# Issuing the exchanges of q's half-row maxima and sums on GpSimd's queue, with another order for the second plan

## The chip, the cores and the metric

The kernel runs on one core of a Trainium2 chip. The metric is the device time in microseconds (us) of one execution. A core has five engines that run side by side, each in its own program order, and wait for one another through semaphores: TensorE (PE, matrix products; its weight loads are shown apart as PEld), VectorE (DVE), ScalarE (ACT), GpSimd (POOL) and SyncE (SP), which here only starts transfers. A transfer can be started by SP, ACT or POOL; "issue" below is the time that the starting engine spends on it, "landing" is the time from the issue to the arrival of its data.

## The reference

```python
def _attn_ref(q, k, v):                       # each 8 x 8 x 576 x 64 (batch, head, sequence, head_dim)
    q_s = np.exp(q - np.max(q, axis=-1, keepdims=True))
    q_s = q_s / (np.sum(q_s, axis=-1, keepdims=True) + 1e-09)
    k_s = np.exp(k - np.max(k, axis=2, keepdims=True))
    k_s = k_s / (np.sum(k_s, axis=2, keepdims=True) + 1e-09)
    kv = np.einsum('bhsd,bhse->bhde', k_s, v)
    return np.einsum('bhsd,bhde->bhse', q_s, kv)

def _moe_ref(x, w_in, w_out):                 # x 4608 x 512, w_in 512 x 2048, w_out 2048 x 512
    h = np.maximum(x @ w_in, 0.0)
    return h * h @ w_out
```

The attention's output, with the heads side by side, is the x of the second function.

## The kernel before, in words

**Work and stages.** The 4,608 rows are nine tiles of 512 tokens. Tile 0 is the first plan's (to about 130 us). Tile 1 (about 130 to 219 us) is a plain feed-forward tile: for each of 16 blocks of the hidden width a product `h` (four slices of x with a block of w_in), on ScalarE and VectorE relu, square and a split in a high part `gh` and a low part `gl`, and then four accumulating products `acc` with w_out. From 219 to about 650 us five steps run two tiles' worth of rows with sums of blocks of w_in and x, so that fewer products are needed; the sums of w_in (`w_sums`) are read from device memory through two buffers, `ring_0` and `ring_1`, with SP's queue. For one pair of hidden blocks the ring loads are a first one of 768 KB into one ring buffer, two of 256 KB, and one of 512 KB. PE multiplies the ring blocks with x sums (`w0` ... `w5`) into two banks, `h_2_0_0` and `h_2_0_1`; ScalarE copies the bank to `u0`, `u1`, `u2`, and only then may PE write the next product into it. The last stage (650 to 805.5 us) is a joint one.

`ring_0` has the memory that `x0` of tile 1 had, so its first load waits for PE's last product that reads `x0_1`: the first six of `h_1_15`. `ring_1` has that of `x1_1`.

**The attention beside it.** While PE multiplies for one tile, the other engines make the attention's output for the next, one pair of heads `p` at a time (four pairs in a batch element `b`). For b of 2 and more q is loaded in blocks of 32 columns: four loads of 72 KB put the two halves of each 64-wide row on different partitions. So each partition has the maximum and the sum of half a row:

- `blocks_exp` takes the half row's maximum (into `bst[:, 0]`), subtracts it and takes the exponential on ScalarE;
- `blocks_swap` sums the half row on VectorE (into `bst[:, 1]`) and starts four transfers of 32 partitions by 36 numbers (4.5 KB), which bring each partition its partner's maximum and sum (into `bst[:, 2:4]`);
- `blocks_norm`, the merge, has VectorE wait for them, then two small VectorE operations, a small exponential on ScalarE, four small VectorE operations and the scaling of q.

There are 24 such exchanges (6 batch elements by 4 pairs), so 96 transfers, all in the second plan.

**The order of work.** The program does not run in the order in which its functions are called. Every operation is recorded as a node (`Engine.tell`, which is why nearly every row of the profile says L101), and `Planner.order` writes the nodes out again: at each step it takes the engine that could start soonest, and on it the node with the largest `tail`, an urgency. `shift` is called once for each number of a list and adds a random amount to the tails of up to 40 nodes in a row; the list thus selects one order out of many:

```python
r = random.Random(seed)
at, size, by = r.randrange(len(self.nodes)), r.randint(1, 40), r.gauss(0.0, 5.0)
for n in self.nodes[at:at + size]:
    n.tail += by
```

`SEEDS` is the list for the first plan, `LATER` that for the second, which has everything from tile 1 to the joint stage.

Of the kernel before, what the change touches and what calls it, by code (L numbers as in the profile page):

```python
# [381 lines left out]
def attention_ffn(  # L382
# [64 lines left out]
    )  # L447
    EASE = 0.0
    EARLY = 2
# [36 lines left out]
    V, S, G = Engine(plan, nc.vector, 0.14, 0.00108, port=2), Engine(plan, nc.scalar, 0.18, 0.00087), Engine(plan, nc.gpsimd, 0.1, 0.0021, 0.23, 1)  # L486
    T, Y = Engine(plan, nc.tensor, 0.013, 1 / 2400, port=None), Engine(plan, nc.sync, 0.1, 0.0)
# [260 lines left out]
    def blocks_swap(b, p):  # L748

        st = made["bst", b, p]  # L750
        V.tensor_reduce(out=st[:, 1, :].only("sum"), in_=made["q", b, p], op=ALU.add, axis=AX.X, n=SQ)
        for j in range(2):
            for a in range(2):
                at, of = j * D + a * Q, j * D + (1 - a) * Q
                Y.dma_start(
                    out=st[at:at + Q, 2:4, :].only(at),
                    in_=st[of:of + Q, 0:2, :].only("max", "sum"), kb=1,
                )
        made["swap", b, p] = True
# [697 lines left out]
    def prepare(b, p, begin=True):  # L1457

        k_max(b, p)
        if b >= TB:  # L1460
            k_reduce(b, p)
            if begin:
                blocks_exp(b, p)
                if p:
                    blocks_swap(b, p)
            k_shift(b, p, made.pop(("kmx", b, p)), V)
            return
        q_max(b, p, G)
        if p == 0:
            tail_exp(b)  # L1470

    def step(b, s):

        p, i = divmod(s, NP)
        if b >= TB:
            if i == 0:
                if ("bst", b, p) not in made:
                    blocks_exp(b, p)
                if ("swap", b, p) not in made:
                    blocks_swap(b, p)  # L1480
            elif i == 1:
                blocks_norm(b, p)
        elif i == 0:
            k_turn_max(b, p)
            q_exp(b, p)
            q_norm(b, p, G)
            if p == 0:
                tail_norm(b)
# [852 lines left out]
```

## Time and profile before

| | before |
|---|---|
| time, median of 3 runs (lowest to highest) | 806.51 us (806.22 to 807.58) |
| the profiled execution | 807.3 us |
| its span, first to last instruction | 805.5 us |
| mean granted TensorE clock | 0.997 |
| instructions | 14938 |

The span is what the profile sees; 1.8 us of the execution lie around it. PE is busy nearly throughout and its clock stays at the upper level, so the reading looks for the few places at which PE stands still, and for what it waits there.

### The profile page before, as it was taken

Reading aid. Unit: us, or ns where it says so; the run is one execution under the profiler, and the core shown is the slowest. Engines: PE = TensorE matmul, PEld = TensorE weight load, DVE = VectorE, ACT = ScalarE, POOL = GpSimd, SP = SyncE. Lnnn points to the kernel's source line nnn. Section 1 sums busy time; section 2 is a strip of 40 time slices with the busy share of each in tenths; the row PEclk is TensorE's granted clock in tenths of the full one; section 3 lists DMA queues with packets and bytes.
Section 4 is the critical chain, followed back from the end, with each engine's and each line's share of the span. In section 5 each row is a group of like instructions: output and inputs, shape, how many; then the busy total and the mean of one; then the engine's idle time right before and its main releaser. Section 6 shows DMA issues by size and latency. Waiting matters only on the chain.

```text
span 805.5 us, 14938 instructions
## 1 busy us (share of the span) xinstructions
PE 786.8 (98%) x5189; PEld 690.0 (86%) x5189; DVE 598.7 (74%) x1252; ACT 497.6 (62%) x967; POOL 138.7 (17%) x165
## 2 busy tenths in 40 slices
PE   7989999999989999999999999999999999999997
PEld 6668788888888989989898989898989888888887
DVE  6878896778767878777887776778786663346995
ACT  5887864545655667575657666666665665566442
POOL 4888893000000000000000000000000000000005
PEclk9999999999999999999999999999999999999999
DMA  9994115955598989898889888889899469999565
GB/s 270 382 319 158 41 40 166 297 172 154 136 284 248 276 253 292 243 271 242 266 256 265 265 218 267 239 277 261 264 269 271 130 211 353 374 330 381 168 183 101
DMA packets 210890, 193.19 MB, mean 240 GB/s; under 512 B 127424, under 2 KB 172992, under 8 KB 210816
## 3 DMA queue, kind: packets, MB, share of 16 engines
q1 hardware_dynamic: 205824, 189.96, 77.3%
q10 hardware_dynamic: 4352, 1.51, 0.8%
q0 software_dynamic: 640, 0.79, 0.5%
q8 instruction: 41, 0.67, 0.3%
q14 instruction: 33, 0.27, 0.1%
HBM read 150.34 MB, written 41.29 MB: 238 GB/s over the span
## 4 chain that ended last, share of the span: by engine, by line
PE 85%; DMA 6%; SPq 3%; DVE 2%; ACT 1%; issue 1%; POOL 1%; ACTq 0%; POOLq 0%; DVEq 0%
PE acc L101 34%; PE h L101 31%; PE h L1354 9%; PE out L2087 6%; PE kv L101 4%; SPq L101 3%; DMA q<-in_q_dram 1%; DMA raw<-in_moe_w_out_dram 1%; DMA raw<-in_moe_w_in_dram 1%; DMA ring<-w_sums 1%; DMA k<-in_k_dram 1%; ACT w L101 1%; DVE w L101 1%; PE x L101 1%; POOL out_dram L101 1%
## 5 line engine op out<-in xcount | busy, mean ns | idle before, releaser
L101 PE MATMUL acc<-w,gh 128*128 128x512 f32 x888 | 266.9, 382 | 3.6 <-ACT o L101 1.8
L101 PEld LDWEIGHTS acc<-w,gh 128*128 128x128 f32 x888 | 154.2, 190 | 23.9 <-issue 4.8
L101 PE MATMUL acc<-w,gl 128*128 128x512 f32 x444 | 168.3, 379 | 0.0
L101 PEld LDWEIGHTS h<-w,ring 128*128 128x128 f32 x1200 | 152.6, 191 | 12.3 <-issue 2.4
L101 PE MATMUL h<-w,ring 128*128 128x256 f32 x1200 | 155.1, 276 | 1.2 <-DVE c L101 0.8
L101 DVE TENSOR_TENSOR c<-h,u 128x256 f32<-128x256 f32 (+1 forms) x144 | 66.9, 467 | 86.6 <-ACT u L101 48.6
L101 ACT ACTIVATE c<-c 128x256 f32<-128x256 f32 (+1 forms) x198 | 116.2, 587 | 22.3 <-DVE c L101 19.1
L101 ACT COPY u<-h 128x256 f32<-128x256 f32 (+1 forms) x144 | 58.6, 407 | 93.7 <-PE h L101 77.7
L101 POOL PARTITION_ALL_REDUCE kmx<-km x24 | 20.2, 840 | 456.3 <-DVE km L101 392.9
L101 PEld LDWEIGHTS acc<-w,gl 128*128 128x128 f32 x444 | 83.9, 189 | 12.0 <-DVE gl L101 0.2
L101 PE MATMUL h<-x,w 128*128 128x512 f32 x384 | 90.6, 383 | 1.1 <-DVE x L101 0.6
L101 PEld LDWEIGHTS h<-x,w 128*128 128x128 f32 x384 | 71.3, 189 | 13.9 <-issue 1.7
L2087 PE MATMUL out<-w,w 128*128 128x512 f32 (+1 forms) x370 | 72.7, 352 | 0.2 <-DVE o L101 0.2
L2087 PEld LDWEIGHTS out<-w,w 128*128 128x128 f32 x370 | 62.7, 190 | 7.8 <-DVE o L101 0.4
L101 DVE TENSOR_TENSOR gl<-c,gh 128x512 fp32r<-128x512 f32 x80 | 55.1, 690 | 13.8 <-ACT gh L101 12.8
L101 PEld LDWEIGHTS h<-w,w 128*128 128x128 f32 x480 | 59.8, 191 | 3.4 <-issue 0.8
L101 PE MATMUL h<-w,w 128*128 128x256 f32 x480 | 61.2, 276 | 0.0
L101 ACT CAST gh<-c 128x512 fp32r<-128x512 f32 x80 | 49.4, 619 | 2.2
L1354 PE MATMUL h<-w,ring 128*128 128x512 f32 x204 | 46.4, 380 | 0.8 <-ACT u L101 0.8
L101 DVE TENSOR_REDUCE bst<-q 128x18 f32<-128x576 f32 x48 | 35.9, 748 | 13.0 <-DMA q<-in_q_dram 9.1
L1354 PEld LDWEIGHTS h<-w,ring 128*128 128x128 f32 x204 | 38.5, 189 | 6.6 <-ACT u L101 1.2
L101 POOL TENSOR_TENSOR w<-w,w 128x512 fp32r<-128x512 f32 x32 | 41.1, 1295 | 5.9 <-ACT w L101 5.8
(183 smaller groups left out, 1087.1 us busy)
## 6 DMA issues: line engine op xcount, KB each, us to landing
ring<-w_sums SPq DMA_DIRECT2D x48, 768.0 KB, 5.9
w<-w_sums SPq DMA_DIRECT2D x48, 512.0 KB, 5.1
ring<-w_sums SPq DMA_DIRECT2D x90, 256.0 KB, 4.6
k<-in_k_dram SPq DMA_DIRECT2D x32, 256.0 KB, 4.6
raw<-in_moe_w_in_dram SPq DMA_DIRECT2D x16, 512.0 KB, 8.6
raw<-in_moe_w_out_dram SPq DMA_DIRECT2D x16, 512.0 KB, 9.6
w<-wo_sums SPq DMA_DIRECT2D x32, 256.0 KB, 3.9
g_b<-c SPq DMA_DIRECT2D x30, 256.0 KB, 5.5
```

The lines of the kernel that those rows point to most:

```text
L101: getattr(self.eng, op)(*map(real, args), **{k: real(a) for k, a in kwargs.items()})
L1354: nc.tensor.matmul(out=out.real(), lhsT=a[:, k * P:(k + 1) * P].real(), rhs=in_turn(m[k]).real(), start=(begin and k == 0 and i == 0), sto ...
L2087: nc.tensor.matmul(out=banks[name][m][:, at].real(), lhsT=a[:, m * P:(m + 1) * P].real(), rhs=(rhs if half is None else rhs[:, half]).real ...
```

## The change

The four transfers of an exchange are started by GpSimd (`G`) in place of SyncE (`Y`), and `LATER` has 27 more numbers:

```diff
@@ LATER
-        1730000948, 1730000978,
+        1730000948, 1730000978, 2220000000, 2220000002, 2220000005, 2220000010, 2220000017, 2220000021,
...
+        2220000287, 2220000317, 2220000402, 2220000438, 2220000516,
@@ blocks_swap
                 at, of = j * D + a * Q, j * D + (1 - a) * Q
-                Y.dma_start(
+                G.dma_start(
                     out=st[at:at + Q, 2:4, :].only(at),
                     in_=st[of:of + Q, 0:2, :].only("max", "sum"), kb=1,
```

Both edits change the order that the planner writes out, on all engines. Three places of it follow. A name ends in the tile or batch element, the pair or block, and a running number that may differ between the two orders.

PE at the end of tile 1, around the last product that reads `x0_1`; before, four rows of `kv` products of attention pairs (2,2) and (2,3) stand between the two halves of `h_1_15`:

```order
L101 MATMUL h_1_15_2465<-x0_1_1603,w14_1474 128x512 x6
L101 MATMUL kv_2_2_2331<-qT_2_2_2248,kv_2_2_2397 64x512
L101 MATMUL kv_2_3_2342<-qT_2_3_2471,kv_2_3_2400 64x512
L101 MATMUL kv_2_2_2331<-qT_2_2_2248,kv_2_2_2397 64x512
L101 MATMUL kv_2_3_2342<-qT_2_3_2471,kv_2_3_2400 64x512
L101 MATMUL h_1_15_2465<-x1_1_1619,w14_1474 128x512 x6
```

The same place after the change:

```order
L101 MATMUL kv_2_2_2335<-qT_2_2_2227,kv_2_2_2410 64x512
L101 MATMUL kv_2_3_2346<-qT_2_3_2435,kv_2_3_2433 64x512
L101 MATMUL kv_2_2_2335<-qT_2_2_2227,kv_2_2_2410 64x512
L101 MATMUL kv_2_3_2346<-qT_2_3_2435,kv_2_3_2433 64x512
...
L101 MATMUL h_1_15_2481<-x0_1_1603,w14_1474 128x512 x6
L101 MATMUL h_1_15_2481<-x1_1_1619,w14_1474 128x512 x6
```

The `kv` rows have moved ahead of the accumulating products of block 12, so that nothing stands between the halves of `h_1_15`.

SP's queue from the first ring load on; `w_sums_0` to `w_sums_2` are the sums of w_in, 128x1536 is the load of 768 KB and 128x512 one of 256 KB. Before:

```order
L101 DMA ring_0_2479<-w_sums_0_1607 128x1536
L101 DMA q_3_0_2488<-in_q_dram 32x18x32 x4
L101 DMA ring_0_2479<-w_sums_0_1607 128x512
L101 DMA ring_1_2527<-w_sums_0_1607 128x512
L101 DMA k_3_1_2531<-in_k_dram 128x2x256
L101 DMA w_sums_4_1822<-sums_i4_1_2416 128x2x256
L101 DMA ring_1_2527<-w_sums_1_1614 128x1536
L101 DMA v_3_1_2566<-in_v_dram 128x4x64 x2
L101 DMA ring_0_2479<-w_sums_2_1757 128x1536
L101 DMA ring_0_2479<-w_sums_1_1614 128x512
L101 DMA bst_3_0_2554<-bst_3_0_2554 32x36 x4
L101 DMA out_0_dram<-o_1_0_2617 128x512
```

And after:

```order
L101 DMA q_3_0_2448<-in_q_dram 32x18x32 x4
L101 DMA k_3_1_2485<-in_k_dram 128x2x256
L101 DMA ring_0_2498<-w_sums_0_1607 128x1536
L101 DMA ring_0_2498<-w_sums_0_1607 128x512
L101 DMA ring_1_2515<-w_sums_0_1607 128x512
L101 DMA ring_1_2515<-w_sums_1_1614 128x1536
...
L101 DMA ring_1_2515<-w_sums_1_1614 128x512
L101 DMA out_0_dram<-o_1_0_2630 128x512
L101 DMA q_3_1_2658<-in_q_dram 32x18x32 x2
L101 DMA out_0_dram<-o_1_2_2665 128x512
L101 DMA q_3_1_2658<-in_q_dram 32x18x32 x2
```

The loads of `q_3_0` have moved ahead of the first ring load, the exchange of pair (3,0) is gone from this queue, and two of the four loads of `q_3_1` stand behind the store of `o_1_2`. On GpSimd's queue the 24 exchanges alternate with the reductions of k's maxima (`kmx`), the only other work that it has in this part of the program.

ScalarE where pair (3,0) is merged (`ACTIVATE bst` is the merge's exponential; `o_1_0` and `o_1_2` are copies that empty the accumulators of tile 1, `acc_1_1` and `acc_1_3` here). Before:

```order
L101 COPY u2_2_0_2611<-h_2_0_0_2534 128x256
...
L101 COPY u0_2_1_2671<-h_2_0_0_2534 128x256
L101 ACTIVATE c0_2_0_2574<-c0_2_0_2574 128x512
L101 ACTIVATE bst_3_0_2554<-bst_3_0_2554 128x2x18
L101 COPY o_1_0_2617<-acc_1_1_1729 128x512
L101 CAST gh_2_0_2691<-c0_2_0_2574 128x512
L101 COPY o_1_2_2653<-acc_1_3_1745 128x512
```

And after:

```order
L101 COPY u1_2_0_2586<-h_2_0_0_2541 128x256
L101 ACTIVATE bst_3_0_2508<-bst_3_0_2508 128x2x18
L101 COPY u2_2_0_2623<-h_2_0_0_2541 128x256
...
L101 COPY u0_2_1_2684<-h_2_0_0_2541 128x256
L101 ACTIVATE c0_2_0_2584<-c0_2_0_2584 128x512
L101 CAST gh_2_0_2694<-c0_2_0_2584 128x512
L101 COPY o_1_0_2630<-acc_1_1_1736 128x512
L101 COPY o_1_2_2665<-acc_1_3_1751 128x512
```

The merge's exponential has moved from behind the first pair's square to a place ahead of the copy `u2_2_0`, and the cast `gh_2_0` to a place ahead of the copy of `acc_1_1`.

## Rows read from the trace of the kernel before

**Rows 1.** The page's busy times of the engines, with share of span and instruction counts.

```profile
PE 786.8 (98%) x5189; PEld 690.0 (86%) x5189; DVE 598.7 (74%) x1252; ACT 497.6 (62%) x967; POOL 138.7 (17%) x165
```

**Rows 2.** PE's waits, 118 to 660 us: us in total, times, longest.

```profile
PE acc L101 <- ACT o L101: 1.8, 1, 1.8
PE h L101 <- DVE c L101: 0.8, 1, 0.8
PE h L1354 <- ACT u L101: 0.8, 1, 0.8
PE h L101 <- DVE gl L101: 0.3, 1, 0.3
```

**Rows 3.** Tile bst, the exchanges' transfers: issue ns min/median/max; landing of all.

```profile
L101 SPq DMA_DIRECT2D bst<-bst x96: 507/588/1364, 138.5 to 624.2; - x96
...
DMA to landing us min/median/max: 1.7/4.0/7.2
```

**Rows 4.** SP's timeline, 213 to 241 us: start us, us, what was issued.

```profile
214.16 0.34 SPq L101 DMA_DIRECT2D ring<-w_sums  x1
214.59 3.78 SPq L101 DMA_DIRECT2D q<-in_q_dram  x4
218.41 1.14 SPq L101 DMA_DIRECT2D ring<-w_sums  x2
...
224.69 3.98 SPq L101 DMA_DIRECT2D bst<-bst  x4
```

**Rows 5.** Issues at 214.2, 218.5 and 224.7 us: KB each, median us to landing.

```profile
ring<-w_sums SPq DMA_DIRECT2D x1, 768.0 KB, 5.0
...
ring<-w_sums SPq DMA_DIRECT2D x1, 256.0 KB, 4.7
...
bst<-bst SPq DMA_DIRECT2D x4, 4.5 KB, 6.5
```

**Rows 6.** PE's timeline, 211 to 235 us: start, us, what [idle before, releaser].

```profile
218.85 0.38 PE L101 MATMUL acc<-w,gl 128*128 128x512 f32 x1
219.32 1.58 PE L101 MATMUL h<-w,ring 128*128 128x256 f32 x12
...
223.21 0.91 PE L101 MATMUL h<-w,ring 128*128 128x256 f32 x6 [0.34 <-DVE gl L101]
...
233.79 0.70 PE L101 MATMUL acc<-w,gh 128*128 128x512 f32 x2 [1.80 <-ACT o L101]
```

**Rows 7.** Chain of waits, 196 to 262 us: start us, us, what it was in.

```profile
210.24 2.59 PE acc L101 x12
...
214.13 1.02 PE kv L101 x8
...
254.64 1.34 PE h L101 x12
```

**Rows 8.** VectorE's timeline, 222 to 234 us: the sum of pair (3,0), the merge's start.

```profile
223.03 0.75 DVE L101 TENSOR_REDUCE bst<-q 128x18 f32<-128x576 f32 x1
...
232.59 0.41 DVE L101 TENSOR_TENSOR bst<-bst 128x18 f32<-128x18 f32 x2 [1.71 <-DMA bst<-bst]
```

**Rows 9.** ScalarE's timeline, 230 to 235 us.

```profile
230.98 0.64 ACT L101 ACTIVATE c<-c 128x512 f32<-128x512 f32 x1
...
233.18 0.57 ACT L101 COPY o<-acc 128x512 f32<-128x512 f32 x1
233.64 0.62 ACT L101 CAST gh<-c 128x512 fp32r<-128x512 f32 x1
```

**Rows 10.** POOL: output stores' issue ns; its reductions, 120 to 640 us; one of them; VectorE beside that.

```profile
L101 POOL DMA_DIRECT2D out_dram<-o x16: 584/584/907, 783.3 to 801.9; - x16
...
L101 POOL PARTITION_ALL_REDUCE kmx<-km x24 | 20.2, 840 | 456.3 <-DVE km L101 392.9 <-DVE v L101 26.6 <-DVE qtail L101 21.0
...
154.90 1.67 POOL L101 PARTITION_ALL_REDUCE kmx<-km  x1 [15.64 <-DVE km L101]
...
154.72 1.28 DVE L101 TENSOR_TENSOR full_i<-w 128x512 f32<-128x512 f32 x2
```

2 rows, old and new, of the table LATER are left out of this document.

## The prediction

> **What bounds the kernel now.** Read the busy times first [rows 1]: PE works 98% of the span, GpSimd 17%. Only PE's idle time, or work that PE has to do more, can move the end. So the second view is the list of PE's waits over the part of the program that the second plan orders and in which the exchanges lie, 118 to 660 us [rows 2]. The reader is to see how little it is: four waits, 1.8 + 0.8 + 0.8 + 0.3 = 3.7 us in 542. No order can win more than this there, 0.5% of the time; and every other exchange, however late, costs PE nothing now. I call a difference of up to 0.2% (1.6 us), about what a measurement of this kernel can tell from no change, "the same".
>
> The third step is to trace each wait to what caused it. The 1.8 us one is the exchange itself. SP issues the four transfers of pair (3,0) at 224.69, taking 3.98 us, behind several ring loads [rows 4]; they land 6.5 us after issue (a median over the four) where the median of all 96 is 4.0 [rows 3, 5]. VectorE, idle 1.71 us for them, starts the merge at 232.59 [rows 8], ScalarE's small exponential stands ahead of the copy that empties `acc_1_1` (233.18, [rows 9]), and PE, ready at 231.99, starts at 233.79 [rows 6]. The 0.3 us one, at 223.21 [rows 6], is labelled with a VectorE operation, but the product also needs the 256 KB ring load, issued at 218.41 behind four loads of q that hold SP for 3.78 us [rows 4], which lands 4.7 us later [rows 5]: 223.1. I take the load as its cause. The 0.8 us ones are the maximum of q_3_1, waiting for its loads ahead of an operation on `c`, at 246 us, and casts ahead of a copy to `u` at 654 us.
>
> **The change part by part.**
>
> *The issue itself.* SP is relieved of 96 issues of 0.588 us [rows 3]. GpSimd's nearest row is its own output stores: 0.584 us each, at most 0.907 [rows 10]. So an exchange takes GpSimd 4 x 0.584 = 2.3 us against SP's 2.4: equal. What is queued behind it on GpSimd is the next pair's reduction of k's maxima; GpSimd idles 456 us ahead of those 24 reductions [rows 10], so 24 x 2.3 = 56 us fit eight times over, and the k side is not what VectorE and PE wait for in [rows 2]. Cost 0; if the cover were gone, 2.3 us an exchange.
>
> *First ring load.* Before, x0's last product ends at 214.13 [rows 7], the load is issued at 214.16 [rows 4] and lands 5.0 us later [rows 5], 219.16. PE fills the time with the kv rows (1.02, [rows 7]), the second half of `h_1_15` and twelve acc products (2.59), is ready at 218.85 + 0.22 = 219.07 and starts at 219.32 [rows 6]: late by 0.25. Afterwards the kv rows stand ahead of x0's last product, so 1.02 us of cover is gone: six products of 0.215 (half of the 2.59 for twelve, 1.29) and the 2.59 are 3.9 us against 5.2 from release to start. Late by 1.3, so **+1.0**. Bounds: the q loads now stand ahead of the ring load, not behind it; landing of 4.0 (the median of exchanges) to 6.5 (the longest in these rows) gives 0 to +2.5.
>
> *Second ring load.* It now follows the first directly, without 3.78 us of q issues in between: due in time, **-0.3**. Bounds -0.3 to 0.
>
> *Exchange (3,0).* The loads of q_3_0 stand earlier, and the sum of the half rows is done by about 219.9 (ScalarE's exponential of q now stands ahead of the high part of `h_1_15`, which PE's ring products must follow closely; an estimate from the order and those times). GpSimd issues to 222.2, landing 2.0 to 4.0 later (between the shortest and the median of [rows 3]) gives 224.2 to 226.2. The merge's exponential stands ahead of the copy `u2_2_0`, and PE needs that copy's bank after the first pair's 30 h products (0.112 each, 1.34 for twelve) and 18 acc products (0.216 each): 7.25 us behind a start at 220.3, 227.5 [rows 7]. Take off two small VectorE operations (0.41, [rows 8]), the small exponential, the copy and the handing over, by estimate 1.1 in all: the merge may start as late as 226.4. It makes it, barely at 4.0: **-1.8**. Bounds: with landing 6.5, 228.7, it is 2.3 late: +0.5; so -1.8 to +0.5.
>
> *Copy of acc_1_1.* The cast `gh_2_0` now stands ahead of it. From the square's end (230.98 + 0.64 = 231.62, [rows 9]) the cast takes about 0.5 (its row says 0.62, of which some overlaps with its neighbours) and the copy 0.57: 232.7, against PE ready at 231.99. PE still waits, **+0.7** of the 1.8 removed. Bounds 0 to +1.8 (another operation ahead as now).
>
> *q_3_1 at 246 us.* Half its loads stand behind a store, and its exponential comes earlier on ScalarE. I cannot place its need better than at the 0.8 that it costs today: **0**, bounds -0.8 to +1.0 (a wait as long as the longest of [rows 2]).
>
> *The wait at 654 us, and the rest.* ScalarE's order before 654 us keeps the same casts: **0**. Between 250 and 650 us PE has no wait now, so a new order can only add: **0** taken, up to +3.6 (two waits as long as the longest of [rows 2]), since a few ring loads now stand behind others.
>
> *Sum:* +1.0 - 0.3 - 1.8 + 0.7 + 0 = -0.4. The profiled execution, 807.3 us, would be 806.9; it is 0.8 above the median of the runs shown (806.51), so the median would be 806.1.
>
> The landing is the weak spot of the exchange's term. Before, the exchange stood in one queue with SP's ring loads of 768 KB; afterwards it has a queue without them. The Trainium skill, page "DMA: Bandwidth & Descriptors", section "Queues, rings and completion order", says that each DMA engine takes turns between the queue rows it has work for, a packet at a time, so that small transfers on their own queue need not stand behind large ones; by it landing would be nearer 2 than 6.5, and the sum would stay at -0.4 with the merge 2 us ahead of its deadline. No run so far shows the exchanges on another queue.
>
> **The rivals.**
>
> *B: the transition clears.* One mechanism: the first ring load finds its queue empty and lands in 4.0, and the copy of acc_1_1 is in time because the pair's square runs earlier without the merge in the way. Terms: 0 - 0.3 - 1.8 + 0 = -2.1, with q_3_1 also earlier -0.8: -2.9, so 803.6 (804.4 without q_3_1). For it: three of the four waits of [rows 2] lie between 219 and 246 us. Against: the 5.0 landing had nothing ahead of it of its own tile.
>
> *C: the new order makes loads late elsewhere.* The same terms, but the first ring load lands in 6.0, between the 5.0 and 6.5 of [rows 5] (+1.0), and two later pairs wait for a ring load behind another (0.8 each, as [rows 2] has them): -0.4 + 1.0 + 1.6 = +2.2, so 808.7, slower. It decides once these added waits pass 2.0 us in all, the 0.4 gained and the 1.6 of the bound. For it: PE has no slack at all between waits. Against: SP has 96 issues fewer, so loads behind it go sooner.
>
> *D: GpSimd's issue is stretched beside VectorE.* One reduction on GpSimd took 1.67 us where the mean is 0.84 [rows 10], while VectorE ran operations with two inputs from SBUF (154.72, [rows 10]). Twice 0.584 is 1.17 an issue, 4.7 an exchange, and with landing 4.0 it is 8.7 us from sum to merge. Before, (3,0) had 8.8 (223.78 to 232.59) and cost 1.8, so 7.0 is free: it decides at 0.75 us an issue. At 8.7 each exchange is up to 1.7 late; if half of 24 cost that, +20; if three do, +5: 811 to 826. Against: 16 stores on GpSimd beside VectorE's last stage have a median of 0.584 and a maximum of 0.907. The Trainium skill, the same page, section "SWDGE vs HWDGE vs iDMA", has a rule against the change: GpSimd writes its descriptors itself, into memory that VectorE can lock it out of, while the hardware queues are spared that. By that rule the price is D's, 811 or more; the trace's stores do not show it.
>
> That the change does nothing is not a case: the order of all engines differs.
>
> **How the numbers follow.** The forecast (A, the same: 806.1, own range 804.9 to 807.6) 42%; B 30%; C 20%; D 8%. The likeliest is A. Faster by over 0.2% (under 804.9) holds B and a tail of A: 0.32. Slower (over 808.1) holds C, D less what C leaves inside the same: 0.26. The rest, 0.42, is the same. The range leaves out D and the outer tails of B and C: 803.3 to 809.0.
>
> **What would show each step.** In the profile after: GpSimd's issues of `bst` at 0.58 us, and landing of 2 to 4 us (steps one and three; 1.2 us or 6.5 us would make D or the failed term right). The first ring product waiting 1.3 us for the ring (+1.0 right) or none (B). At the copy of acc_1_1 a wait of 0.7 or none. At the second ring load no wait. PE's idle between 250 and 650 us, zero now, tells A from C at once. The prediction is wrong if PE's sum of idle in 118 to 660 us is under 2.1 or above 5.3 us, or if PE's work itself grows, which the order gives no reason for.

## The result, and the profile after

The changed kernel takes 812.55 us (median of 5 runs, 810.88 to 814.81) against 806.22 (5 runs, 803.34 to 807.58): a ratio of 1.0092, 95% interval 1.0071 to 1.0113. It is slower by 6.3 us, outside the range of the forecast. The profiled execution takes 814.0 us with a span of 812.2.

PE is not where the time went. The page's busy times after, which answer to [rows 1]:

```profile
PE 787.7 (97%) x5189; PEld 690.5 (85%) x5189; DVE 599.7 (74%) x1252; ACT 498.0 (61%) x967; POOL 186.6 (23%) x261
```

PE's waits from 118 to 660 us after, which answer to [rows 2]:

```profile
PE acc L101 <- ACT o L101: 1.0, 2, 0.8
PE h L101 <- DMA ring<-w_sums: 0.8, 1, 0.8
PE acc L101 <- DVE gl L101: 0.4, 1, 0.4
PE h L101 <- ACT kt L101: 0.4, 1, 0.4
PE h L1357 <- ACT u L101: 0.3, 1, 0.3
PE h L101 <- DVE c L101: 0.2, 1, 0.2
```

They add up to some 3.1 us, from 3.7. So the next view is PE's timeline at the very end; its last row before, and then after:

```profile
795.50 5.62 PE L2087 MATMUL out<-w,w 128*128 128x256 f32 x48 [0.22 <-DVE o L101]
```

```profile
794.90 5.62 PE L2090 MATMUL out<-w,w 128*128 128x256 f32 x48 [0.20 <-DVE o L101]
```

PE's last product ends at 801.12 before and at 800.52 after, 0.6 us earlier. In this execution PE was ahead by more than that before the changed part began (a row of 36 `h` products of tile 1 starts at 134.23 us against 135.63), so its later part is no faster. The span ends at 805.5 and at 812.2. Thus from PE's last product to the end it is 4.4 us before and 11.7 after: all of the loss, and a little more, lies where no product is left. What runs there belongs to the line that ends the program. Its instructions on GpSimd and SyncE (durations in ns, min/median/max; first and last start in us), before:

```profile
L2336 POOLq DRAIN  x3: 40/102/2824, 801.9 to 805.2; - x3
L2336 SPq DRAIN  x3: 7/7/7, 804.4 to 805.0; - x3
```

And after:

```profile
L2339 POOLq DRAIN  x3: 40/102/10148, 801.3 to 812.0; - x3
L2339 SPq DRAIN  x3: 7/7/7, 803.8 to 811.7; - x3
```

Each engine ends with a drain instruction, and all wait for one another behind it: SyncE's last drain starts at 805.0 before and at 811.7 after, 0.3 us behind the end of GpSimd's first. GpSimd's takes 2.82 us before and 10.15 after, 7.3 us more, while SyncE is through with its first at 803.8. The last store does not explain it. GpSimd's timeline has its issue beside the drain's start, at 801.31 after, and the trace has its data landed at 803.25, 8.2 us before the drain ends (at 811.44):

```profile
801.31 0.58 POOL L101 DMA_DIRECT2D out_dram<-o  x1 [2.10 <-DVE o L101]
```

The exchanges themselves, tile bst after (answers to [rows 3]):

```profile
L101 POOL DMA_DIRECT2D bst<-bst x96: 496/497/767, 137.1 to 624.9; - x96
...
DMA to landing us min/median/max: 1.5/4.4/6.7
```

An issue takes 0.497 us, less than SyncE's 0.588, and at most 0.767. Landing is 4.4 us in the median against 4.0.

Three rows of PE's timeline after show the moved places at the end of tile 1; they answer to [rows 6]:

```profile
218.67 1.57 PE L101 MATMUL h<-w,ring 128*128 128x256 f32 x12 [0.80 <-DMA ring<-w_sums]
...
222.76 0.94 PE L101 MATMUL h<-w,ring 128*128 128x256 f32 x6 [0.22 <-DVE c L101]
...
232.40 0.70 PE L101 MATMUL acc<-w,gh 128*128 128x512 f32 x2 [0.82 <-ACT o L101]
```

And VectorE's start of the merge of pair (3,0), which waits for nothing now (answers to [rows 8]):

```profile
223.92 0.41 DVE L101 TENSOR_TENSOR bst<-bst 128x18 f32<-128x18 f32 x2
```

### The profile page after: what moved, and what is told of

The parts are those of the page before. It is cut to its first block, busy times and chain, and to the rows that moved or that the text cites. A ratio compares the mean times of both kernels' runs of the same rounds, so it can differ in the third digit from the quotient of the medians.

```text
span 812.2 us, 14978 instructions
## 1 busy us (share of the span) xinstructions
PE 787.7 (97%) x5189; PEld 690.5 (85%) x5189; DVE 599.7 (74%) x1252; ACT 498.0 (61%) x967; POOL 186.6 (23%) x261
## 3 DMA queue, kind: packets, MB, share of 16 engines
q0 software_dynamic: 3712, 1.24, 0.8%
## 4 chain that ended last, share of the span: by engine, by line
PE 87%; DMA 4%; ACT 3%; SPq 1%; DVE 1%; issue 1%; POOL 1%; POOLq 0%; DVEq 0%; ACTq 0%
PE acc L101 34%; PE h L101 31%; PE h L1357 9%; PE out L2090 7%; PE kv L101 4%; DMA raw<-in_moe_w_out_dram 2%; DMA k<-in_k_dram 2%; SPq L101 1%; ACT c L101 1%; PE x L101 1%; ACT w L101 1%; ACT gh L101 1%; POOL out_dram L101 1%; DVE w L101 0%; ACT raw L101 0%
## 5 line engine op out<-in xcount | busy, mean ns | idle before, releaser
L101 POOL DMA_DIRECT2D bst<-bst x96 | 48.0, 506 | 266.1 <-DVE bst L101 229.7
L101 PEld LDWEIGHTS acc<-w,gl 128*128 128x128 f32 x444 | 83.9, 189 | 12.8 <-DVE gl L101 1.0
```

The source lines that it names most:

```text
L101: getattr(self.eng, op)(*map(real, args), **{k: real(a) for k, a in kwargs.items()})
```

## The experiments

**Theory one** after the first reading: GpSimd's drain retires every transfer that GpSimd issued, at a price for each, 7.3 us for 96 more; until the end of the program nobody pays it. "Retire" is only a name here for what the drain does about a transfer: no trace shows what that is, only how long it takes. **Rivals**: the new order delays the last stores; a fixed price once GpSimd issues transfers in mid-program; a price by packets or bytes. Four kernels test the first two, and three more the last.

*The new numbers without the move* (after):

```diff
-                G.dma_start(
+                Y.dma_start(
```

> The exchanges go back to SyncE's queue, the 27 new numbers stay. Theory one (the last instruction of GpSimd, a drain, must retire every transfer that GpSimd issued, so that its length grows with their number: 7.3 us for 96 more, 0.076 each): with 20 transfers on GpSimd the drain is 2.8 us as before, and the end lies 4.4 us behind PE's last product; time by PE's own waits, 804 to 807. Rival (the order that the new numbers give delays the last stores or their landing): the drain stays near 10 us and the time near 812.

Measured: 815.61 us, 1.0138 (1.0119 to 1.0157) of before. The drain:

```profile
L2339 POOLq DRAIN  x3: 40/93/2811, 811.5 to 814.8; - x3
```

It is 2.81 us, and the end follows PE's last product by 4.3 us: theory one holds and the rival of the late stores falls. The time was missed by 9 us, and PE shows why: from the first ring product to the first product of the joint output it takes 515.4 us (219.26 to 734.62), against 505.7 before (219.32 to 725.01) and 505.8 after (218.67 to 724.43). The 27 numbers, applied to nodes on other engines, give a third order and no part of the changed one.

*The move without the new numbers* (before):

```diff
-                Y.dma_start(
+                G.dma_start(
```

> The exchanges go on GpSimd's queue, the 27 new numbers are left out. Theory one: drain 10.1 us, some 7 us more than before, whatever PE's order gives; time 811 to 816. Rival (the new order): drain 2.8 us, time within 2 us of before.

Measured: 818.8 us, 1.018 (1.0155 to 1.0204).

```profile
L2336 POOLq DRAIN  x3: 40/102/10148, 805.7 to 816.3; - x3
```

The drain is that of after to the nanosecond, under another order. Here PE takes 510.6 us between the same two marks (218.16 to 728.78), 4.9 more than before; the new numbers win that back.

*Half of the transfers on each queue* (after):

```diff
-                G.dma_start(
+                (G, Y)[j].dma_start(
```

> Of the four transfers of an exchange two stay on GpSimd, two go to SyncE: 48 + 20 = 68 on GpSimd. Theory one: if the price of each adds to the last landing, the drain is 2.8 + 48 x 0.076 = 6.5 us; if it runs beside that landing from the drain's start, 68 x 0.0875 = 5.9 us (10.15 by 116). Rival (a fixed price once GpSimd has issued transfers early, such as a ring that is set up or wrapped): 10 us again, or 2.8.

Measured: 813.11 us (one run).

```profile
L2339 POOLq DRAIN  x3: 40/102/6228, 804.3 to 811.0; - x3
```

Between 116 transfers (10.15) and 68 (6.23) lie 3.92 us, 0.082 each. Behind the last store's issue (which ends 0.60 after the drain's start) it is 9.54 = 116 x 0.0823 and 5.62 = 68 x 0.0827: proportional to the number. The rival of a fixed price falls. The 20 transfers of before do not lie on this line: their 2.22 us behind the last issue are more than 20 x 0.082 = 1.6. There the drain ends 0.87 us behind the landing of the last store, as it does in the two other runs that have 20 to retire at the end (the new numbers alone, and the run that follows). So with few transfers the length of the drain no longer tells their number.

*One drain more, early in the joint stage, where GpSimd is idle* (after):

```diff
+        if s == 2 * J:
+            nc.gpsimd.drain()
         if s == 3 * J:
```

> After, with one more drain on GpSimd early in the joint stage, where it idles for 127 us. Theory one: the early drain takes some 7 us, hidden, and the last one only has the 20 stores: 2.8 us; the end 7 us earlier than after, 804 to 806, 0.6 us below before by the profiled ends of PE's work. Rival (the drain's length is a state of the queue or counts all transfers of the program, not those since the last drain): the last drain stays at 10 us, time 812.

Measured: 804.71 us (11 runs) against 804.7 of before on the same chip: 1.0003 (0.9991 to 1.0016). The early drain, the one operation that it first waits out, and the closing drains:

```profile
L2283 POOLq DRAIN  x1: 10402/10402/10402, 651.0 to 651.0; - x1
```

```profile
651.09 2.43 POOL L101 TENSOR_TENSOR w<-x,w 128x512 fp32r<-128x512 f32 x1 [28.03 <-ACT w L101]
```

```profile
L2341 POOLq DRAIN  x3: 46/102/2825, 799.2 to 802.5; - x3
```

The 2.43 us operation ends at 653.52 and the drain at 661.44: 7.92 us for 96 transfers, 0.0825 each, though the last of them had landed at 624.09. So the drain does not wait for a landing there. It is hidden behind PE, the closing drain is back at 2.83, the end follows PE's last product by 4.4 us as before, and the whole loss is gone, though the exchanges are still on GpSimd and PE, ScalarE, GpSimd and SyncE run all their other instructions in the order of after. This is the cause of the 6.3 us, shown by removing it alone.

Three further kernels ask what the price counts, and whether it can be hidden otherwise.

*Each transfer of an exchange cut in two* (after):

```diff
-                G.dma_start(
-                    out=st[at:at + Q, 2:4, :].only(at),
-                    in_=st[of:of + Q, 0:2, :].only("max", "sum"), kb=1,
-                )
+                for i in (0, Q // 2):
+                    G.dma_start(
+                        out=st[at + i:at + i + Q // 2, 2:4, :].only(at + i),
+                        in_=st[of + i:of + i + Q // 2, 0:2, :].only("max", "sum"), kb=1,
+                    )
```

> After, with each transfer of an exchange cut in two of 16 partitions: 192 + 20 = 212 transfers on GpSimd, with as many packets in all (3,712) as after. Theory one (a price for each transfer): the last drain, 5.62 us for 68 and 9.55 for 116 behind the last store's issue, is 0.0823 each: 0.6 + 212 x 0.0823 = 18.0 us. Rival (a price for each packet): 10.1 us, as after.

Measured: 863.71 us (one run; in the order for twice the issues PE stands idle for 38 us between 130 and 720 us), and

```profile
L2340 POOLq DRAIN  x3: 40/102/8110, 853.0 to 861.7; - x3
```

Neither 18.0 nor 10.1. Theory one falls in the form "every transfer waits for the drain". The trace also has 6,784 packets on GpSimd's queue, not the 3,712 that I took: a transfer of 16 partitions makes 32 as well. 8.11 - 0.60 = 7.51 us are 91 transfers, so 121 of 212 were retired before. GpSimd's timeline shows where; in 24 exchanges one alone starts late:

```profile
490.80 3.83 POOL L101 DMA_DIRECT2D bst<-bst  x8 [19.76 <-DVE bst L101]
501.77 0.70 POOL L101 PARTITION_ALL_REDUCE kmx<-km  x1 [7.15 <-DVE km L101]
514.31 3.85 POOL L101 DMA_DIRECT2D bst<-bst  x8 [11.83 <-DVE w L101]
...
535.45 3.85 POOL L101 DMA_DIRECT2D bst<-bst  x8 [3.72 <-DVE bst L101]
```

VectorE's sum of that exchange:

```profile
510.34 0.75 DVE L101 TENSOR_REDUCE bst<-q 128x18 f32<-128x576 f32 x1
```

It ends at 511.09; the issue starts 3.22 us later, where the 23 others have 0.29 to 0.31. It is the 129th transfer. When GpSimd retires the 121 stays open. At 494.14, when it issues the 128th, 120 have landed, which would fit the number; but from there 9.9 us (121 x 0.082) would end at 504.6, and the reduction at 501.77 runs in between in its usual 0.70 us, while the issue at 514.31 is still late. The idle stretch ahead of that issue, 11.8 us, has room for the 9.9; but by then all 128 have landed (the last at 497.08), and 121 is not explained.

*The loads of q on GpSimd, the exchanges on SyncE* (before):

```diff
                 at = (j ^ p % 2) * D + a * Q
-                Y.dma_start(
+                G.dma_start(
                     out=t[at:at + Q].only(at),
```

> Before, with the 96 loads of q's blocks of columns (72 KB each, 576 packets each) started by GpSimd and the exchanges left on SyncE: 116 transfers on GpSimd again, with some 18 times the packets and 16 times the bytes of each. Theory one (a price for each transfer, whatever it carries): the last drain is 10.1 us. Rival (packets or bytes count): well over 20 us. The time of the whole is not forecast, since the order changes with the engine.

Measured: 833.79 us (one run), and

```profile
L2336 POOLq DRAIN  x3: 46/102/3610, 827.6 to 831.7; - x3
```

Both guesses missed. The trace gives 5,248 packets, 48 for each load of 72 KB (not the 576 that I took) beside 32 for each store in the mean. The last run's limit, 128 transfers of 32 packets, is 4,096 packets; here that is full within the 22nd group of four loads. If the 84 loads ahead of that group are retired there, 12 x 48 + 20 x 32 = 1,216 packets are left, and at 9.55 us for 3,712 that is 3.1 + 0.6 = 3.7 us, against 3.61. This fits, worked out afterwards, and no issue in this trace shows where they are retired. A limit of 128 transfers does not fit, since there are only 116. Nor do bytes: the kernel after and the run before this one both move 1.24 MB on this queue, and their drains are 10.15 and 8.11 us. Whether the price goes by transfer or by packet stays open: the 32 transfers left would give 3.2 us by the first, 3.7 by the second.

*The last stores on SyncE and ScalarE alone* (after; all six lists of queues):

```diff
-(Y, S, G)
+(Y, S)
-(Y, G)
+(Y, S)
```

> After, with the 20 last stores that GpSimd issues given to SyncE and ScalarE. GpSimd's last work is then an operation that ends near 656 us, and its closing drain (96 x 0.082 = 7.9 us) runs beside PE's last stage. Theory one: the closing drain is some 8 us, ends near 664 us, and the end follows PE's last product by 4 to 5 us; time 804 to 806. Rival (the end is held up by something else of the exchanges on GpSimd, which the early drain happened to clear): time stays at 812.

Measured: 815.76 us, 1.0139 (1.0111 to 1.0167).

```profile
L2339 POOLq DRAIN  x3: 40/102/10406, 651.7 to 813.0; - x3
```

GpSimd's closing drain starts at 651.7, takes the 10.41 of the early drain (the same operation ahead of it), and the end follows PE's last product by 3.9 us: on the drain theory one was right. The time was not: ScalarE's casts and copies for PE's last products now stand behind stores that wait, and from 787 to 802 us PE waits 6.3 us for operations of ScalarE and VectorE, where it waits 0.2 after. ScalarE's timeline:

```profile
794.88 0.93 ACTq L101 DMA_DIRECT2D out_dram<-o  x2
795.93 1.04 ACT L101 CAST w<-w 128x1024 fp32r<-128x1024 f32 x1 [5.89 <-issue]
...
799.85 1.07 ACT L101 COPY x_joint<-out 128x512 f32<-128x512 f32 x2 [2.88 <-DVE o L101]
```

Those copies ran at 790.38 in the kernel after; PE's last product ends at 809.41.

**Theory two**: when 128 transfers of 32 packets are outstanding GpSimd retires those that have landed, some 121 of them, before its next drain and at the same price; the drain pays for the rest. It makes a forecast that looks odd: a few transfers more than in the kernel after, and a short drain. So the last kernel cuts the transfers of the last eight exchanges alone (after):

```diff
+                n = Q // 2 if b >= 6 else Q
+                for i in range(0, Q, n):
-                G.dma_start(
-                    out=st[at:at + Q, 2:4, :].only(at),
-                    in_=st[of:of + Q, 0:2, :].only("max", "sum"), kb=1,
+                    G.dma_start(
+                        out=st[at + i:at + i + n, 2:4, :].only(at + i),
+                        in_=st[of + i:of + i + n, 0:2, :].only("max", "sum"), kb=1,
```

> After, with the transfers of the last 8 exchanges alone cut in two of 16 partitions: 64 + 64 = 128 of the exchanges and 20 stores, 148 on GpSimd. First theory (each transfer since the last drain is retired by the next drain, 0.082 us each): 0.6 + 148 x 0.082 = 12.8 us of closing drain. Second theory, formed on the run with 212 transfers (a drain of 8.1 us means 91 left of 212, so 121 were retired before, and the one late issue, 3.22 us behind its sum where all others are 0.29, is the 129th): when 128 are outstanding GpSimd retires those that have landed by itself; the 128th is here the last exchange, some 630 us, where GpSimd idles, so that some 121 are retired there unseen and 27 are left: the closing drain is 0.6 + 27 x 0.082 = 2.8 to 3.0 us, the end 4.4 to 4.7 us behind PE's last product, though more transfers were issued than in after.

Measured: 819.77 us (one run, by PE's order: its last product ends at 813.10), and

```profile
L2341 POOLq DRAIN  x3: 40/102/3023, 813.9 to 817.4; - x3
```

3.02 us, and the end 4.6 us behind PE's last product: theory two, not 12.8. It shows that most of the 148 were retired before the drain, not how many: the 20 stores alone would take 2.8.

## Why the prediction was wrong

**The step that failed** is "*The issue itself.* ... So an exchange takes GpSimd 4 x 0.584 = 2.3 us against SP's 2.4: equal ... Cost 0". It took the price of a transfer to be its issue. The issue came out cheaper still (0.497), and the cover was there, but a transfer from GpSimd has a second price of 0.082 us that is paid later, and 116 of them (9.54 us, against 2.22 for the 20 of before) came due at once behind the last store, where nothing covers them: +7.3 us on the closing drain. The sum added its terms to the profiled execution's time and so took all that follows PE's last product as unchanged.

It could have been looked for. In the profile of before the chain that ended last has GpSimd's queue at its end:

```profile
801.89 0.60 POOLq L2336
```

And GpSimd's closing drain ended 2.2 us behind its last issue, later than SyncE's. An engine that closes the program already, and gets 96 transfers more, was worth a term with an unknown price. The argument "only PE's idle time, or work that PE has to do more, can move the end" left out what runs when PE is done. The prediction's own signs had the same gap: it was to be wrong if PE's idle time left 2.1 to 5.3 us, and that came to 3.1, well inside, in a kernel that is 6.3 us slower.

**The terms that were summed** held, by rows. First ring load: PE was late by 0.25 and is now by 0.95, of which 0.80 is a wait for the load (+1.0 forecast, +0.7 came); it lands 4.5 us after its issue, not 5.0. Second ring load: it lands in time, as forecast, but the product now waits 0.22 for an operation on `c`, so 0.34 became 0.22 (-0.3 forecast). Exchange (3,0): VectorE no longer waits and neither does PE (-1.8, as forecast), though not by a shorter landing: its transfers took 4.2 to 5.1 us, above the 2 to 4 that was taken, and the sum of the half rows ended at 217.85, 2 us earlier than the estimate. The copy of `acc_1_1`: 0.82 (+0.7 forecast). q_3_1 at 246 us: gone (0 forecast, -0.8 as the bound). At 654 us: 0.3 from 0.8, but 0.4 more at 651.64, where there was no wait (0 forecast, 0 in all). Between 250 and 640 us two waits of 0.4 and 0.2 where there was none (0 taken, +3.6 the bound). In all -0.6 on PE's waits against -0.4. In time this is nothing that can be measured: with the closing drain out of the way the kernel stands at 1.0003 (0.9991 to 1.0016) of before. Case A's sum of PE's terms was right in size; its end was not.

**The rivals.** D has the measured time in its range (811 to 826) by luck, with the wrong mechanism: its price was an issue of 1.17 us, and the issues took 0.497 in the median and 0.767 at most; the landing was 4.4. Its sentence on the Trainium skill, page "DMA: Bandwidth & Descriptors", section "SWDGE vs HWDGE vs iDMA", therefore stays unshown here: with VectorE busy for 74% of the span none of the 96 issues shows a stall of that kind. What the prediction drew from the section "Queues, rings and completion order" of the same page, that the exchanges would land nearer to 2 us on a queue of their own, is not borne out either: 4.4 us after against 4.0 before. C did not happen: the new waits between 250 and 640 us sum to 0.6 us, under the 2.0 at which it would decide, and neither is for a ring load. Of B's three conditions one came, q_3_1's wait; the ring load and the copy of `acc_1_1` still make PE wait.

## What to carry to other kernels

A transfer issued by GpSimd is not paid when it is issued: here 0.082 us of it wait for GpSimd's next drain, at the latest behind the program's last store, so count GpSimd's transfers since the last drain, and put a drain where GpSimd idles (here 7.9 us of it ran unseen beside PE, and the closing drain was 7.3 us shorter). Read the chain's last link and each engine's closing instructions before adding work to an engine, however idle it is on average. And a list of random numbers that selects an order belongs to one program: each half of this change alone was slower (1.014 and 1.018) than both together (1.009), so undoing halves did not split the effect.

## What the runs showed of the hardware

- GpSimd's drain took 0.082 us for each transfer of 32 packets issued since its last drain: 68 in 5.62 us, 96 in 7.92, 116 in 9.54, the same whether the last had landed 27 us before the drain began or landed during it. With 20 it took 2.22 us, 0.11 each, and ended 0.87 us behind the last landing.
- With more transfers outstanding the drain got shorter: 8.11 us for 212, 3.02 for 148, 3.61 for 116 that were larger. All three fit a limit of 4,096 packets, at which GpSimd retires by itself some 120 of the 128; the 3.02 was forecast from it (2.8 to 3.0). That the limit is one of packets and not of transfers rests on the run with q's loads alone; and when and how GpSimd retires is not seen in the trace, but for one issue that started 3.22 us late.
- A small transfer on GpSimd's own queue landed no sooner (a median of 3.8 us in the order with the old numbers, 4.4 with the new) than on the queue that carries the ring loads (4.0 and 3.8).
